# Attention features, then hash-routed experts on one core: each expert's weights loaded one place earlier, and turned outputs joined and scattered three steps later

## The chip, the cores and the metric

The kernel runs on one core of a Trainium2 chip. The metric is the device time of one execution in microseconds (us), as the median of several runs. The engines are named as in the profile: PE (TensorE matmuls), PEld (its weight loads), DVE (VectorE), ACT (ScalarE), POOL (GpSimd) and SP (SyncE, which here only issues DMAs).

## The reference

Two blocks follow each other. The first is attention without a softmax, over 4 batches, 4 heads, 1088 positions and head size 32, all in float32:

```python
def phi(x):
    a = np.einsum('rd,bhsd->bhsr', S1, x)          # r = 8
    b = np.einsum('rd,bhsd->bhsr', S2, x)
    return np.einsum('bhsi,bhsj->bhsij', a, b).reshape(*x.shape[:-1], r * r)
q_p, k_p = phi(q), phi(k)
kv = np.einsum('bhsf,bhsd->bhfd', k_p, v)
z = np.sum(k_p, axis=2)
num = np.einsum('bhsf,bhfd->bhsd', q_p, kv)
den = np.einsum('bhsf,bhf->bhs', q_p, z)[..., None] + 1e-06
x = (num / den).transpose(0, 2, 1, 3).reshape(B * S, H * D)   # 4352 rows of 128
```

The second sends each of the 4352 rows to one of 8 experts by its token id, and runs the expert's two layers (w1 is 128 x 1024, w2 is 1024 x 128):

```python
expert_idx = token_ids * np.int64(2654435761) % np.int64(8)
for e in range(8):
    mask = expert_idx == e
    h = np.maximum(x[mask] @ w1[e], 0.0)
    out[mask] = h @ w2[e]
```

## The kernel before

**Attention.** A loop goes over the four batches `b`. PE turns q and k, multiplies them by S1 and S2, turns the features, and forms kv and the numerators; DVE forms the features (L532), ACT evicts, POOL copies v into place (`values`, L552) and divides (`x_main`, L623; `x_tail`, L629). SP loads q, k and v (`load_main`, L122) and stores the rows of x to a DRAM tensor `x_rows` (`x_rows`, L634; `x_tail_rows`, L638). While `b` is 0 and 1, the routing is computed: `order` (L366) holds the experts by rank, `get` and `put` the rows to gather and to scatter.

**Experts.** The rows of an expert are cut into an early group of 256 (rows of the first two batches) and a late group of 320 or fewer, so there are 16 groups; `by_turn` is the order in which they are worked: 0, 1, 2, 3, 4, 8, 5, 9, 6, 10, 7, 11 to 15. A group takes eight steps `c`, one for each 128 columns of the hidden layer. In a step PE does layer 1 of this group (`layer1`, L918, into one of four PSUM banks), ACT or DVE evicts it with the relu (L648, L650, every other step), and PE does layer 2 of the group ahead (`layer2`, L926). So the step of a group is fixed by PE while the banks come free in time.

**Rows in and out.** `fetch_tile` gathers 128 rows by an indirect DMA from POOL (L642); its index is copied by DVE just ahead (`paced`, L709), which sets when the gather may go. The first tiles are turned on PE (`bring`, L720; `bring_tile`, L726). From the fourth group on, DVE splits the rows into 16-bit halves (`turn_in`, L734), a DMA transpose from SP turns them (L735), and DVE joins them (`join_in`, L740). Outputs go the other way: at the end of a group ACT copies the two halves (`out_columns`, L966), SP issues two DMA transposes one group later (`turn_out`, L979), DVE joins them (`join_out`, L987), and POOL scatters 128 rows at a time by an indirect DMA (`scatter_next`, L929).

**Weights.** `load_expert(r, layers, ahead)` reads the expert of rank r into a register of SP (L135) and loads whole layers (512 KB each, L143 and L147); `ahead` is a small write to the tile, on ACT or DVE, that the load has to wait for, so that it goes no earlier than that engine reaches that point. `load_half` loads half a layer (256 KB) behind a memset of DVE (L155, L159).

**Order.** Every engine works through one queue, in the order in which the program text issues its instructions (a manual schedule). In the expert part the table `beside` gives what is issued next to PE's steps: `at(g, c, f)` puts f behind step c of the group in turn g. For the step of the joins:

```python
for g in range(2, G - 1):
    at(g, 1, turn_out, by_turn[g - 2])
    c = FC if g < E else 5
    for i, f in enumerate((join_out, scatter_next, scatter_next, scatter_next)):
        at(g + (c + i) // FC, (c + i) % FC, f)
```

FC and E are both 8: for g below 8, join_out stands at step 0 of the next group, and the scatters at its steps 1 to 3.

Of the kernel before, what the change touches and what calls it, by code (L numbers as in the profile page):

```python
# [30 lines left out]
def kernel(  # L31
# [17 lines left out]
    E, _, F = moe_w1.shape  # L49
# [10 lines left out]
    FC = F // P  # L60
# [53 lines left out]
    def load_main(src, b, tag, ahead=None):  # L114
        t = load.tile([P, H, T, D], F32, tag=tag, name=f"{tag}{b}")
        if ahead:
            ahead(t[:, 0, 0, 0:1])
        rows = src[b, :, 0:SM, :].rearrange("h (p t) d -> p h t d", t=T)
        parts = {(0, "k"): H, (0, "q"): H, (0, "v"): H // 2}.get((b, tag), 1)
        for i in range(parts):  # L120
            hs = slice(i * H // parts, (i + 1) * H // parts)
            nc.sync.dma_start(t[:, hs], rows[:, hs])  # L122
        return t
# [8 lines left out]
    def load_expert(r, layers=(1, 2), ahead=None, eng=nc.sync, eng_type=ENG.SP):  # L132

        if r not in at_rank:
            _, es = nc.values_load_multi_w_load_instructions(  # L135
                order[0:1, r:r + 1], engines=(eng_type,), min_val=0, max_val=E - 1,
                skip_runtime_bounds_check_because="a count of the experts ahead of one of them is below their number")
            at_rank[r] = es[0]
        e = at_rank[r]
        if 1 in layers:  # L140
            if ahead:
                ahead(w1[:, r, 0:1])
            eng.dma_start(w1[:, r], moe_w1[bass.ds(e, 1)].rearrange("o p f -> p (o f)"))  # L143
        if 2 in layers:
            if ahead and 1 not in layers:
                ahead(w2[:, r, 0, 0:1])
            eng.dma_start(w2[:, r], moe_w2[bass.ds(e, 1)].rearrange("o (c p) d -> p (o c) d", p=P))  # L147
# [195 lines left out]
    def route_bases(cnt):  # L343

        less = const.tile([P, E], F32, name="less")
        nc.vector.scalar_tensor_tensor(less[:], took[:], is_late[:], cnt[:, 0], op0=OP.mult, op1=OP.add)
        base = const.tile([P, E], F32, name="base")
        nc.vector.scalar_tensor_tensor(base[:], place[:], float(1 << RB), less[:], op0=OP.mult, op1=OP.add)
        nc.vector.tensor_tensor(seq[:], seq[:], base[:].unsqueeze(2).to_broadcast([P, E, C]), op=OP.add)
# [66 lines left out]
    def hot(dst, numbers, values):  # L416

        _, n, w = dst.shape
        nc.vector.tensor_tensor(dst.rearrange("p c (n x) -> p c n x", x=2),
                                numbers.rearrange("p (n x) -> p n x", x=2).unsqueeze(1).to_broadcast([P, n, w // 2, 2]),  # L420
                                values.unsqueeze(2).to_broadcast([P, n, w // 2, 2]), op=OP.is_equal)

    def route_rows(part):
        c = slice(part * C // 2, (part + 1) * C // 2)
        hot(row1[:, c], number[:], st[:, 1, c])
# [57 lines left out]
    def turned_all(src, which):  # L483
        sT, half = turned(src, which)
        for g in range(GQ):
            nc.scalar.copy(sT[:, g], half(g)[:])
        return sT
# [93 lines left out]
    def q_turned(f, engs):  # L581

        fT = work.tile([P, T, H // 2, P], F32, tag="fT", name="fT", bufs=1)
        for i, eng in enumerate(engs):
            copy_of(eng)(fT[:, 2 * i:2 * i + 2], f_turned(f, i)[:])
        return fT
# [80 lines left out]
    turn_of = {g: i for i, g in enumerate(by_turn)}  # L667
# [80 lines left out]
    A, V = nc.scalar, nc.vector  # L748
# [50 lines left out]
    for b in range(B - 1):  # L799
        last = b == B - 2  # L800
        if b > 1:
            kT = turned_all(k_t[b + 1], "kT")
        if b == 1:
            q_t.append(load_main(q, 3, "q", A.memzero))
        if last:
            qT = turned_all(q_t[b + 1], "qT")
        fT = q_turned(f, (A, A, A, A) if b > 0 else EVICT)
        if b == 0:
            route_bases(cnt)
            digits = route_ranks()  # L810
            tail_ps = bank([P, 2, TT, P], "tail_ps")
            tail_turned(k_tail, tail_ps, 0)
            tail_turned(q_tail, tail_ps, 1)
            tailT = work.tile([P, 2, TT, P], F32, tag="tailT", name="tailT", bufs=1)
            nc.scalar.copy(tailT[:], tail_ps[:])
            qT = turned_all(q_t[1], "qT")
            for u, va_tail in enumerate(va_tails):
                rows = tail_rows(u * TT)
                nc.gpsimd.tensor_copy(va_tail[rows, :, :, 0:D], v_tail[rows])
            tail_features(tail_products(tailT))  # L820
            route_parts(digits)
            route_order_end()
        elif not last:
            qT = turned_all(q_t[b + 1], "qT")
        if b == 1:
            v_t.append(load_main(v, 2, "v", A.memzero))
            route_in_tile()
        if last:
            idx = route_list()
            route_end(idx)  # L830
        if b > 0:
            kv = kv_products(b, kp, range(T + 1))
            m = kv_diagonal(b, kv)
        if b == 1:
            route_tiles_p()
        if last:
            load_expert(0, (1,), A.memzero)
        abq, aq, f = ab_bank(), first_of_ab(), feature_tile("f")
        s_products(abq, qT, range(GQ))
        first_copied(aq, abq, range(GQ))  # L840
        abk, ak, kp = ab_bank(), first_of_ab(), feature_tile("kp")
        s_products(abk, kT, range(GQ))
        first_copied(ak, abk, range(GQ))
        if b == 0:
            q_t.append(load_main(q, 2, "q", A.memzero))
            kT, half = turned(k_t[2], "kT")
            nc.scalar.copy(kT[:, 0], half(0)[:])
            kv_products(0, None, range(T, T + 1), kv)
            m = kv_diagonal(0, kv)
            tail_f_turned()  # L850
            nc.scalar.copy(kT[:, 1], half(1)[:])
        values(b + 1)
        if b == 1:
            v_t.append(load_main(v, 3, "v", A.memzero))
            route_rows(0)
            route_tiles()
            route_rows(1)
            denominators(0)
            x_main_all(0)
            for g in range(GQ):  # L860
                x_rows(0, g)
            x_tail_rows(0)
        features(f, aq, abq, range(GQ))
        if b == 0:
            route_slots()
        x_products(b, fT, m)
        x_tail_products(b, m)
        if b == 0:
            k_t.append(load_main(k, 3, "k", A.memzero))
        if last:  # L870
            load_expert(0, (2,), A.memzero)
        if b == 0:
            features(kp, ak, abk, range(GQ))
        elif last:
            features(kp, ak, abk, range(GQ))
            denominators(b)
        else:
            denominators(b)
            features(kp, ak, abk, range(GQ))
        if 0 < b and not last:  # L880
            x_main_all(b)
        if b == 1:
            for g in range(GQ):
                x_rows(1, g)
            x_tail_rows(1)
        if last:
            for j in range(tiles_of(0)[1]):
                fetch_tile(0, j, True)

    e = B - 1  # L890
    fT = q_turned(f, EVICT)
    load_expert(1, (1,), A.memzero)
    for j in range(2):
        fetch_tile(1, j)
    kv = kv_products(e, kp, range(T // 2))
# [141 lines left out]
    def at(g, c, f, *a):  # L1037
        beside.setdefault((g, c), []).append(lambda: f(*a))
# [12 lines left out]
    for j in range(tiles_of(1)[1]):  # L1051
        at(0, 5 + j, bring_tile, 1, j)
    at(1, 5, bring, 2)
    for r in range(2, E):
        for x in range(2):
            at(turn_of[r] - 1, 3 * x, load_half, r, 2, x)
            if r > 2:
                at(turn_of[r] - 2, 4 + 3 * x, load_half, r, 1, x)


    ahead = [(k, j) for k in by_turn[4:11] for j in range(tiles_of(k)[1])]
# [3 lines left out]
    assert not ahead  # L1065

    gate = nc.vector.memset
    at(0, 1, load_expert, 1, (2,), lambda x: gate(x, 0.0))
    at(0, 5, load_expert, 2, (1,), lambda x: gate(x, 0.0))
    for i in range(GQ):  # L1070
        at(0, 5 + i, x_main, e, i, nc.gpsimd)
        at(1, 1 + i, x_rows, e, i)
# [7 lines left out]
        at(i - 1, 4, join_in, by_turn[i])  # L1080
    for g in range(2, G - 1):
        at(g, 1, turn_out, by_turn[g - 2])
        c = FC if g < E else 5
        for i, f in enumerate((join_out, scatter_next, scatter_next, scatter_next)):
            at(g + (c + i) // FC, (c + i) % FC, f)
        if g == G - 4:

            at(g, 7, nc.gpsimd.drain)
        if g == G - 3:
            at(g + 1, 0, nc.gpsimd.drain)  # L1090
# [17 lines left out]
    g, lo = G - 1, size_of(G - 1) - P  # L1108
# [40 lines left out]
    with tc.If(turns > 0):  # L1149
        with tc.For_i(0, turns):  # L1150
# [19 lines left out]
            at = moe.tile([P, C], F32, tag="at", name="at", bufs=1)  # L1170
# [70 lines left out]
```

## Time and profile before

| | us |
|---|---|
| median of 3 runs | 178.63 (178.38, 178.63, 179.55) |
| profiled execution, its own time | 180.15 |
| its span | 178.1 |
| PE busy | 170.3 |
| PEld busy | 143.0 |
| DVE busy | 96.2 |
| POOL busy | 93.0 |
| ACT busy | 67.9 |
| DMA, mean | 145 GB/s over the span |

The span goes from the first to the last instruction of the profiled execution; what lies around it belongs to the start and end of the program. Busy times are shares of different stages: attention takes the first 52 us, the expert groups the rest. A row of a timeline gives the start, the duration, the engine, the line, the operation with its output and input, a count, and in brackets the idle time of the engine ahead of it and what ended it. A row of waits gives who waited for whom, the sum in us, how often, and the longest. In a row of windows the numbers are the length, then busy time and count of PE, PEld, DVE, ACT and POOL, the granted PE clock, the DMA share and GB/s.

### The profile page before, as it was taken

To read this page: it belongs to the slowest core of one execution; us is meant where nothing else is said; L and a number is where in the kernel's file an instruction comes from. 1 tells how busy PE (TensorE), PEld (TensorE's weight loads), DVE (VectorE), ACT (ScalarE), POOL (GpSimd) and SP (SyncE) were. 2 spreads that over 40 slices of the span, in tenths; PEclk is the share of its full clock that TensorE was granted. 3 is DMA by queue.
4 is the path that set the end of the run, shared out by engine and by line. 5 is a ranking of instruction groups with operands and counts; after the bars stand their busy time and mean duration, and the time that the engine had idled before them with its cause. 6 is when DMAs were issued, how large, how long until landed. Compare 5 with 4: busy or idle time off the path is not lost. (4 is left out here: it accounts for less than half of the span.)

```text
span 178.1 us, 4354 instructions
## 1 busy us (share of the span) xinstructions
PE 170.3 (96%) x1571; PEld 143.0 (80%) x1571; DVE 96.2 (54%) x311; ACT 67.9 (38%) x183; POOL 93.0 (52%) x134
## 2 busy tenths in 40 slices
PE   7899999999999999699999999999999999999990
PEld 3689999999888888588777778788888777778990
DVE  3688998997944423364444343633457562442330
ACT  3548686846453232132341323133141332321330
POOL 7314342775258465077776612775655760406752
PEclk9999999999999999999999999999999999999997
DMA  4897249554668679894992683386342522210111
GB/s 141 239 279 219 86 137 309 157 196 156 196 233 235 223 183 199 165 289 102 230 170 74 184 173 74 103 216 140 79 96 52 117 65 54 54 37 29 43 36 32
DMA packets 39398, 25.83 MB, mean 145 GB/s; under 512 B 20980, under 2 KB 35573, under 8 KB 39376
## 3 DMA queue, kind: packets, MB, share of 16 engines
q1 hardware_dynamic: 36960, 20.98, 47.5%
q0 software_dynamic: 2240, 4.53, 8.9%
q8 instruction: 13, 0.21, 0.5%
q10 hardware_dynamic: 176, 0.04, 0.1%
q14 instruction: 9, 0.07, 0.1%
HBM read 17.41 MB, written 4.52 MB: 123 GB/s over the span
## 5 line engine op out<-in xcount | busy, mean ns | idle before, releaser
L926 PE MATMUL op<-hT,w 128*128 128x256 f32 (+8 forms) x256 | 76.3, 389 | 0.0
L650 DVE TENSOR_SCALAR hT<-hp 128x256 f32<-128x256 f32 (+9 forms) x68 | 29.1, 428 | 56.2 <-PE hp L918 53.4
L926 PEld LDWEIGHTS op<-hT,w 128*128 128x128 f32 x256 | 47.5, 190 | 10.5
L648 ACT ACTIVATE hT<-hp 128x256 f32<-128x256 f32 (+9 forms) x68 | 26.6, 391 | 64.4 <-PE hp L918 62.7
L929 POOL DMA_INDIRECT out_dram<-os,put x35 | 35.3, 1008 | 28.0 <-DVE os L987 11.4
L642 POOL DMA_INDIRECT xg<-x_rows,idx x33 | 34.0, 1031 | 28.7 <-DVE idx L709 19.0
L918 PE MATMUL hp<-xT_late,w 128*128 128x320 f32 (+8 forms) x144 | 41.7, 385 | 0.0
L918 PE MATMUL hp<-xT,w 128*128 128x256 f32 x128 | 37.7, 382 | 1.6 <-DVE idx L709 1.6
L918 PEld LDWEIGHTS hp<-xT,w 128*128 128x128 f32 x128 | 23.8, 190 | 7.5 <-DVE idx L709 2.0
L918 PEld LDWEIGHTS hp<-xT_late,w 128*128 128x128 f32 x144 | 25.3, 190 | 4.7
L532 DVE TENSOR_TENSOR f<-first_of_ab,ab_ps 128x1024 f32<-128x1024 f32 x8 | 9.3, 1205 | 1.8 <-ACT first_of_ab L525 1.8
L987 DVE COPY os<-turned 128x256 uint16<-128x256 uint16 (+1 forms) x26 | 7.4, 329 | 5.3 <-DMA turned<-half 5.3
L532 DVE TENSOR_TENSOR kp<-first_of_ab,ab_ps 128x1024 f32<-128x1024 f32 x8 | 9.3, 1209 | 0.9 <-ACT first_of_ab L525 0.9
L561 PE MATMUL kv<-va,kp 128*64 128x33 f32 x256 | 8.5, 224 | 0.1
L561 PEld LDWEIGHTS kv<-va,kp 128*64 128x64 f32 x256 | 7.9, 138 | 0.8 <-issue 0.4
L734 DVE COPY xh<-xg 128x256 uint16<-128x256 uint16 (+1 forms) x26 | 7.1, 316 | 2.2 <-DMA xg<-x_rows,idx 2.2
L597 PE MATMUL x_ps<-m,fT 128*64 128x66 f32 x256 | 8.3, 222 | 0.0
L597 PEld LDWEIGHTS x_ps<-m,fT 128*64 128x64 f32 x256 | 7.8, 137 | 0.5 <-issue 0.5
L966 ACT COPY half<-op 128x256 uint16<-128x256 uint16 x16 | 5.2, 375 | 7.5 <-PE op L926 7.5
L578 PE MATMUL fT_ps<-ident,f 128*128 128x128 f32 x64 | 7.9, 275 | 0.0
L552 POOL COPY va<-v 128x1024 f32<-128x1024 f32 (+1 forms) x4 | 3.7, 934 | 7.9 <-DMA v<-in_v_dram 4.1
L578 PEld LDWEIGHTS fT_ps<-ident,f 128*128 128x128 f32 x64 | 7.0, 140 | 0.3
(199 smaller groups left out, 166.3 us busy)
## 6 DMA issues: line engine op xcount, KB each, us to landing
w<-in_moe_w_dram SPq DMA_DIRECT2D x22, 256.0 KB, 4.5
w<-in_moe_w_dram SPq DMA_DIRECT2D x5, 512.0 KB, 5.4
x_rows<-xs SPq DMA_DIRECT2D x8, 256.0 KB, 3.1
k<-in_k_dram SPq DMA_DIRECT2D x3, 512.0 KB, 5.8
q<-in_q_dram SPq DMA_DIRECT2D x3, 512.0 KB, 4.9
v<-in_v_dram SPq DMA_DIRECT2D x3, 512.0 KB
out_dram<-os,put POOLq DMA_INDIRECT x35, 2.6
xg<-x_rows,idx POOLq DMA_INDIRECT x33, 3.5
```

The costliest lines, as they stand in the source:

```text
L532: nc.vector.tensor_tensor(dst[:].rearrange("p t h i j -> p (t h) i j")[:, r], a[:, r].unsqueeze(3).to_broadcast(shape), rows_of_ab(ab)[:, ...
L561: nc.tensor.matmul(kv[h * R * R:(h + 1) * R * R, pr], f[:, 2 * pr + h].rearrange("p i j -> p (i j)"), v_[:, 2 * pr + h], start=(t == 0 and ...
L578: nc.tensor.transpose(p[:, t, pr], f[:, 2 * i + t, 2 * pr:2 * pr + 2].rearrange("p h i j -> p (h i j)"), ident[:])
L597: nc.tensor.matmul(p[r, t, 2 * pr:2 * pr + 2].rearrange("p h d -> p (h d)"), fT[:, lo + t, pr, r], m[:, pr].rearrange("p h d -> p (h d)"), ...
L642: nc.gpsimd.indirect_dma_start(out=dst, out_offset=None, in_=x_dram[0:rows], in_offset=bass.IndirectOffsetOnAxis(ap=idx, axis=0), bounds_c ...
L648: nc.scalar.activation(dst, src, AF.Relu if relu else AF.Copy)
L650: return nc.vector.tensor_scalar(dst, src, 0.0, None, op0=OP.max).ins
L734: nc.vector.tensor_copy(xh[:, x * w:(x + 1) * w], _half(xg3[k][:].rearrange("p a b -> p (a b)")[:, 0:w], x))
L918: nc.tensor.matmul(hp[:, 0:hi - lo], w1[:, g % E, c * P:(c + 1) * P], x_columns(first_of(g) + lo, first_of(g) + hi), start=True, stop=True)
L926: nc.tensor.matmul(ops[g][:, 0:hi - lo], w2[:, g % E, c], hTs[g][:, c, lo:hi], start=(c == 0), stop=(c == FC - 1))
L929: st_ = nc.gpsimd.indirect_dma_start(out=out[:], out_offset=bass.IndirectOffsetOnAxis(ap=idx, axis=0), in_=src, in_offset=None, bounds_che ...
L987: nc.vector.tensor_copy(_half(os[:].rearrange("p a b -> p (a b)"), x)[:, 0:n * DM], tts[x][:, 0:n].rearrange("p a b -> p (a b)"))
```

## The change

The loads of the first experts' layers each take the place in the order where the layer ahead of them was loaded. The first layer of rank 0 has a new place, behind the load of the fourth v, without a gate. Rank 2 is now loaded in two whole layers, and halves begin with rank 3, whose first layer takes steps 0 and 3 of turn 1. Joins and scatters of the outputs with g below 8 go from steps 0 to 3 to steps 3 to 6 of the next group.

```diff
         if last:
-            load_expert(0, (1,), A.memzero)
+            load_expert(0, (2,), A.memzero)
...
         if b == 1:
             v_t.append(load_main(v, 3, "v", A.memzero))
+            load_expert(0, (1,))
             route_rows(0)
...
         if last:
-            load_expert(0, (2,), A.memzero)
+            load_expert(1, (1,), A.memzero)
...
     fT = q_turned(f, EVICT)
-    load_expert(1, (1,), A.memzero)
+    load_expert(1, (2,), A.memzero)
...
-    for r in range(2, E):
+    for r in range(3, E):
         for x in range(2):
             at(turn_of[r] - 1, 3 * x, load_half, r, 2, x)
-            if r > 2:
-                at(turn_of[r] - 2, 4 + 3 * x, load_half, r, 1, x)
+            at(turn_of[r] - 2, (4 if r > 3 else 0) + 3 * x, load_half, r, 1, x)
...
-    at(0, 1, load_expert, 1, (2,), lambda x: gate(x, 0.0))
-    at(0, 5, load_expert, 2, (1,), lambda x: gate(x, 0.0))
+    at(0, 1, load_expert, 2, (1,), lambda x: gate(x, 0.0))
+    at(0, 5, load_expert, 2, (2,), lambda x: gate(x, 0.0))
...
-        c = FC if g < E else 5
+        c = FC + 3 if g < E else 5
```

## The prediction

> **What bounds the kernel now.** I read four views in this order: busy times, waits of TensorE, timelines of the engines around the one long wait, and the DMA row there.
>
> ```profile
> PE 170.3 (96%) x1571; PEld 143.0 (80%) x1571; DVE 96.2 (54%) x311; ACT 67.9 (38%) x183; POOL 93.0 (52%) x134
> ```
> ```profile
> PE hp L918 <- DVE idx L709: 1.6, 1, 1.6
> PE idle L225 <- POOL warm L180: 1.0, 1, 1.0
> PE ab_ps L510 <- ACT qT L756: 0.2, 1, 0.2
> ```
>
> TensorE (PE) is busy in 170.3 of 178.1 us, and its list of waits has three entries, 2.8 us together. In the expert part its matmuls stand at an even step (0.43 us for one of 128x256), so busy is real there. The last matmul begins at 173.3; the 4.5 us behind it are the last copy, the last scatters and their landing. So only one thing can be won inside the program: the 1.6 us wait of L918. The waits view blames an index copy (L709), which takes 0.1 us; the true holder stands two lines ahead of it in VectorE's (DVE's) timeline:
>
> ```profile
> 73.86 0.31 DVE L987 COPY os<-turned 128x256 uint16<-128x256 uint16 x1 [4.67 <-DMA turned<-half]
> 74.34 0.31 DVE L987 COPY os<-turned 128x256 uint16<-128x256 uint16 x1 [0.17 <-DMA turned<-half]
> 74.55 0.42 DVE L650 TENSOR_SCALAR hT<-hp 128x256 f32<-128x256 f32 x1
> ```
> ```profile
> 72.86 0.59 PE L926 MATMUL op<-hT,w 128*128 128x256 f32 x2
> 75.02 0.70 PE L918 MATMUL hp<-xT,w 128*128 128x256 f32 x2 [1.56 <-DVE idx L709]
> ```
> ```profile
> 66.33 2.46 SPq L979 DMA_TRANSPOSE turned<-half  x2
> ```
>
> The first join_out stands at the start of group 3, in VectorE's in-order queue. From 69.2 it waits 4.67 us for the first turned output; behind it are the evictions (L650) that give PSUM banks back. PE lives on its four banks until 73.46, then stands 1.56 us. VectorE could be held for 73.46 - 69.2 = 4.3 us before it cost anything.
>
> Why was that transpose late? It was issued at 66.33 and its reader went on at 73.86, while the queue list gives 2.8 us from issue to landing as the median of these transposes. The DMA view for 70 to 74 us (40 slices of 0.1 us) shows the reason:
>
> ```profile
> DMA  3243949994999199099000000000000006999299
> GB/s 110 82 67 59 243 85 248 205 405 26 70 169 120 41 31 187 0 20 5 0 0 0 0 0 5 5 10 10 10 10 10 10 10 200 292 302 225 26 276 348
> ```
>
> From 72.0 to 73.3 hardly a packet starts although SyncE (SP) has transposes and weights outstanding. All queues stand. I see this once; it is not a load that the order of the code forces.
>
> **How the profiled run stands to the median.** Its own time is 180.15, its span 178.1, so 2.05 us lie around the span. The runs shown have 178.38, 178.63 and 179.55. The profiled one is 1.52 us above the median, and the gap is 1.56 us: the likeliest reading is that the median run has next to no gap, that the 179.55 run has most of it, and that a standstill comes in some executions only. The reading against it: a profiled execution may be longer for its own reasons, and then the median has the gap too. This choice is the largest one in the forecast.
>
> **The change part by part.**
>
> *Join and scatter three steps later.* In groups 3 to 8, L987 and the scatters (L929) go from steps 0 to 3 to steps 3 to 6. In group 3, step 3's L918 is at 71.56; after its eviction, two index copies and the turn_in copies (L734, 0.6 us) the join stands at about 73.1, not 69.2: 3.9 us later. Same instructions, same 0.31 us each; nothing added. Even if the turned output still came at 73.86, VectorE would be held 0.8 us plus 0.5 us for the second half, against 4.3 us that the banks cover: the PE gap goes, -1.56 us. What is late next: join_in of group 4 (L740, now behind the join) must be done before group 4 begins, at 68.97 + 6.9 = 75.9. In the profiled run its transpose was issued at 69.53 and the copies ran at 76.01, but behind the held VectorE; the transpose's median landing (3.4 us) gives 72.9, and with the standstill I estimate 75, so 0 to 0.4 us come back in such a run. On POOL, the gathers that stood behind the held index copies (5.5 us idle until 75.30) issue ahead of the scatters, so its run of back-to-back issues, 1.3 us each until 99.8, gets shorter. Scatters go 2.6 us later. Group 3 has four gathers and two scatters, 7.8 us of POOL in 6.9, so 0.9 us runs over; from group 4 on there are four or five issues, at most 6.5 us, in groups of 6.9 to 7.8, so they fit. The last groups (step 5) are untouched, so the tail does not move by itself.
>
> *Weights one place earlier.* 8.4 MB before and after; whole loads go from 5 to 6, halves from 22 to 20: one SP issue (0.38 us) and two memsets (0.06 us) fewer, both off PE's path. No weight is waited for now (no L918 or L926 wait on w), so arriving earlier is worth nothing directly. Indirectly: the half of expert 3's first layer at 65.24 and its register load leave the place ahead of the first turn_out. By the issue times (0.4 + 0.3 for the load and its gate, 0.5 for the register load, the rest waiting) L979 moves from 66.33 to about 64.8, and 256 KB less are ahead of it. That is a second cover of 1.5 us for the same wait; it cannot be won twice.
>
> *The first load behind the fourth v.* SP issues that v at 31.6 and then stands until 34.34 for POOL's xs. The new register load (0.27 to 0.80 us in the trace; order has been there since 21.4) and one issue (0.34) fit in: 0 us. On the queue, 512 KB now come ahead of x_rows(0) and x_rows(1), whose landing releases the first gather:
>
> ```profile
> 35.00:40.00 5.00, 5.00 (x128) 4.79 (x128) 4.86 (x11) 2.55 (x7) 4.01 (x6) 1.00 0.55 203
> ```
> ```profile
> 41.91 1.29 POOL L642 DMA_INDIRECT xg<-x_rows,get  x1 [1.86 <-DMA x_rows<-xs_tail]
> 43.50 1.00 POOL L642 DMA_INDIRECT xg<-x_rows,get  x1 [0.30 <-issue]
> ```
> ```profile
> 46.81 0.44 PE L720 MATMUL xp<-ident,xg 128*128 128x128 f32 x2
> ```
>
> These 5 us moved 203 GB/s at a DMA share of 0.55 (second number from the end). Adding 512 KB needs 308 GB/s, and the page's row has 309 in its best slice of 4.45 us. So 0 us if the queue takes it. If 203 GB/s were its limit, the 512 KB would take 2.6 us more; the second gather lands near 43.5 + 2.5 = 46.0 and PE needs it at 46.81, so 0.8 us are free and PE would stand 1.8 us. A gain is excluded, PE doesn't wait here. Value 0.1 us (the share is far from 1, and x_rows(1) is issued only at 37.7, when most has drained); ends 0 and +1.8. After that the second layer of expert 0, as large, stands where the first did (40.76), and so on: 0.
>
> *Sum* on the profiled execution: -1.56 + 0.1 + 0 to 0.4 gives about 178.8 of 180.15. On the median, where by my reading the gap is mostly absent, the change removes what lifts some runs above the fastest (178.38): **178.2**, with the few tenths it takes from the spread.
>
> **A rule against the change.** The Trainium skill, Advanced Engine Details and Errata, section X-Bar Transpose (TRN2), has transposes as fast as ordinary DMAs, 350 to 400 GB/s. By it the pair of 64 KB transposes needs an estimated 0.4 us of transfer, the output is there by about 70, VectorE is held 1 us of the 4.3 that are covered, and a later join gains 0. The row says 73.86 and a gain of 1.56. I take the row for the profiled run, but the rule describes the run without a standstill, which I hold for the typical one.
>
> **Rivals.**
> 1. The gap is in the typical run as well. For it: all of it is written out in program order, late transposes recur (L987 waits three times, 5.3 us), and a profile may cost its own 1.5 us. Against it: 1.52 against 1.56. Then 178.63 - 1.56 = 177.1, or down to 176.4 if the shorter POOL backlog and earlier transposes also remove later waits.
> 2. Slower: the early 512 KB delay x_rows, hence the gather, and PE waits at bring(0) (L720 at 46.81). It decides from 0.8 us of delay on. At 203 GB/s: 178.4 + 1.8 = 180.2; if the second layer's 512 KB then also stand in the gather's way, 1 us more, 181. For it: nothing there has more than 0.8 us of slack. Against it: the free DMA share of 0.45.
> 3. It doesn't do what it says: the standstill catches join_in of group 4 or a gather, and PE stands elsewhere. 178.6. For it: 75 against 75.9 is tight.
>
> **How the numbers follow.** Forecast 0.42 (177.8 to 178.8), rival 1 0.33, rival 2 0.15, rival 3 0.10. A measurement here tells about 1% from no change, 1.8 us. Faster by over 1% (below 176.8): two thirds of rival 1 at its lower end and a little of the forecast, 0.25. Slower by over 1% (above 180.4): most of rival 2, its upper part and mishaps on the same path, 0.12. The rest, 0.63, within. The range goes from rival 1's lower end, 176.3, to the entry of rival 2's upper part, 180.3.
>
> **What would show it.** Right: no wait of PE on L918 near 73, L987 of the first output at about 73 and its wait under 1 us, L979 first at about 64.8, the first load of w at about 33, the gather still near 42 and L720 near 46.8 without idle. Wrong: an idle entry ahead of L720 (rival 2); a new PE wait at the start of group 4 (rival 3); unprofiled runs that all fall by 1.5 us (rival 1), which would mean that the gap was in every run and my reading of the 1.52 us was a coincidence.

## The result and the profile after

The change takes 179.47 us (median of 20 runs, 178.67 to 182.72), the kernel before, run beside it, 179.18 (20 runs, 178.38 to 180.43). The ratio is **1.001, interval 0.9989 to 1.003**: no difference. In this ratio and in those below, the few longest runs of a kernel are left out (of the change the four from 181.38 us on). The profiled execution of the change has 179.0 us as its own time and a span of 177.2, against 180.15 and 178.1 before.

The first row of the page after, with the busy time of each engine, and then the list of PE's waits (who waited for whom, sum in us, times, longest):

```profile
PE 170.0 (96%) x1571; PEld 142.9 (81%) x1571; DVE 95.8 (54%) x309; ACT 67.7 (38%) x183; POOL 93.4 (53%) x134
```
```profile
PE idle L225 <- POOL warm L180: 1.0, 1, 1.0
PE s_ps L284 <- DVE s_rep L275: 0.4, 1, 0.4
PE xp L726 <- DMA xg<-x_rows,idx: 0.3, 1, 0.3
PE ab_ps L510 <- ACT qT L756: 0.2, 1, 0.2
```

The 1.6 us that L918 waited for L709 are gone from the list. A new entry stands there: `bring_tile` (L726), which turns the first rows of expert 1, waits 0.3 us for a gather. (The 0.4 us of L284 lie at the start of the program.) Behind line 855 the numbers of the changed kernel are one higher, up to the last groups: L919 is the old L918, L980 the old L979, L988 the old L987. DVE's timeline shows the first join, where the kernel before was held 4.67 us:

```profile
73.07 0.15 DVE L709 COPY idx<-get 128x1 int32<-128x1 int32 x1
73.90 0.52 DVE L988 COPY os<-turned 128x256 uint16<-128x256 uint16 x2
74.32 0.14 DVE L709 COPY idx<-get 128x1 int32<-128x1 int32 x1
```

There is no bracket behind L988: no wait is laid to it. It stands 4 us later in the order, behind the index copies, and its outputs are there. The standstill of the DMA queues is not gone. The DMA view of the change for 68 to 74 us, 40 slices of 0.15 us:

```profile
DMA  0066212599999999990001005995965977999899
GB/s 20 1 164 191 82 34 68 160 283 335 345 335 400 295 227 106 147 41 2 7 9 27 0 3 70 143 243 166 298 96 150 219 218 218 410 437 396 328 369 437
```

From 70.7 to 71.6 hardly a byte moves, as before from 72.0 to 73.3. PE waits for nothing there now. The loss is 20 us earlier. PE's timeline of the kernel before, then of the change, where expert 1's tiles are turned between the matmuls of layer 1:

```profile
51.79 1.99 PE L918 MATMUL hp<-xT,w 128*128 128x256 f32 x8
53.62 0.27 PE L726 MATMUL xp<-ident,xg 128*128 128x128 f32 x1
...
54.27 1.26 PE L918 MATMUL hp<-xT,w 128*128 128x256 f32 x4
```
```profile
51.63 1.99 PE L919 MATMUL hp<-xT,w 128*128 128x256 f32 x8
53.92 0.33 PE L726 MATMUL xp<-ident,xg 128*128 128x128 f32 x1 [0.29 <-DMA xg<-x_rows,idx]
...
54.79 1.26 PE L919 MATMUL hp<-xT,w 128*128 128x256 f32 x4
```

From the eight matmuls to the four behind both turns it is 54.27 - 51.79 = 2.48 us before and 54.79 - 51.63 = 3.16 after: 0.68 us lost, though the list of waits shows only 0.3 of them. The last group of matmuls (L1137), of the kernel before, then of the change:

```profile
171.64 1.95 PE L1137 MATMUL op_rows<-w,hT 128*128 128x128 f32 x16
```
```profile
170.33 1.95 PE L1137 MATMUL op_rows<-w,hT 128*128 128x128 f32 x16
```

From the first L726 to this row there are 118.02 us before and 116.41 in the change. With the joins alone (e1 and e8, below) there are 116.19 in both profiles. So in these profiles the late joins take 1.83 us off this stretch, a little more than the one wait in the list; the weights cost 0.22 of it and another 0.45 ahead of L726 (53.92 - 46.66 against 53.62 - 46.81). The change was 0.15 ahead at L720, and 1.83 - 0.22 - 0.45 + 0.15 = 1.31 us remain between these two executions. The medians show none of it.

### The profile page after: what moved, and what is told of

It is laid out like the page before. It is cut to its first block, busy times and chain, and to the rows that moved or that the text cites. A ratio compares the mean times of both kernels' runs of the same rounds, so it can differ in the third digit from the quotient of the medians.

```text
span 177.2 us, 4349 instructions
## 1 busy us (share of the span) xinstructions
PE 170.0 (96%) x1571; PEld 142.9 (81%) x1571; DVE 95.8 (54%) x309; ACT 67.7 (38%) x183; POOL 93.4 (53%) x134
## 5 line engine op out<-in xcount | busy, mean ns | idle before, releaser
L642 POOL DMA_INDIRECT xg<-x_rows,idx x33 | 34.5, 1047 | 21.3 <-DVE idx L709 12.1
L919 PE MATMUL hp<-xT_late,w 128*128 128x320 f32 (+8 forms) x144 | 41.7, 385 | 0.0
L919 PE MATMUL hp<-xT,w 128*128 128x256 f32 x128 | 37.7, 381 | 0.0
L919 PEld LDWEIGHTS hp<-xT_late,w 128*128 128x128 f32 x144 | 25.3, 190 | 4.7
L919 PEld LDWEIGHTS hp<-xT,w 128*128 128x128 f32 x128 | 23.9, 191 | 5.5 <-ACT hT L648 0.4
L561 PE MATMUL kv<-va,kp 128*64 128x33 f32 x256 | 8.4, 224 | 0.1
L561 PEld LDWEIGHTS kv<-va,kp 128*64 128x64 f32 x256 | 7.9, 138 | 0.8 <-issue 0.4
L597 PE MATMUL x_ps<-m,fT 128*64 128x66 f32 x256 | 8.3, 222 | 0.0
L597 PEld LDWEIGHTS x_ps<-m,fT 128*64 128x64 f32 x256 | 7.8, 137 | 0.5 <-issue 0.5
L988 DVE COPY os<-turned 128x256 uint16<-128x256 uint16 (+1 forms) x26 | 7.3, 324 | 1.6 <-DMA xg<-x_rows,idx 1.0
L734 DVE COPY xh<-xg 128x256 uint16<-128x256 uint16 (+1 forms) x26 | 7.0, 313 | 1.2 <-DMA xg<-x_rows,idx 1.0
```

The source lines that it names most:

```text
L561: nc.tensor.matmul(kv[h * R * R:(h + 1) * R * R, pr], f[:, 2 * pr + h].rearrange("p i j -> p (i j)"), v_[:, 2 * pr + h], start=(t == 0 and ...
L597: nc.tensor.matmul(p[r, t, 2 * pr:2 * pr + 2].rearrange("p h d -> p (h d)"), fT[:, lo + t, pr, r], m[:, pr].rearrange("p h d -> p (h d)"), ...
L642: nc.gpsimd.indirect_dma_start(out=dst, out_offset=None, in_=x_dram[0:rows], in_offset=bass.IndirectOffsetOnAxis(ap=idx, axis=0), bounds_c ...
L734: nc.vector.tensor_copy(xh[:, x * w:(x + 1) * w], _half(xg3[k][:].rearrange("p a b -> p (a b)")[:, 0:w], x))
L919: nc.tensor.matmul(hp[:, 0:hi - lo], w1[:, g % E, c * P:(c + 1) * P], x_columns(first_of(g) + lo, first_of(g) + hi), start=True, stop=True)
L988: nc.vector.tensor_copy(_half(os[:].rearrange("p a b -> p (a b)"), x)[:, 0:n * DM], tts[x][:, 0:n].rearrange("p a b -> p (a b)"))
```

## The experiments

Kernels that are compared ran on one chip, one after the other, with the kernel before among them; there are five such groups. In the first two the kernel before took 179 to 180 us, in the three later ones 190 to 192, and every kernel took longer there. One chip is in both conditions (179.42, and later 190.31). So numbers are compared within a group, and ratios are to the kernel before in the same group.

### First condition: the parts alone

**The joins alone**, twice (e1, e8): in the kernel before

```diff
-        c = FC if g < E else 5
+        c = FC + 3 if g < E else 5
```

> Only the joins and scatters three steps later; weights as before. Theory 'two parts cancel': the late turned output no longer holds VectorE, so the profile has no wait of PE on L918 near 73 and no wait ahead of the expert 1 tiles (L726), and the runs lose the part that lifts them above the fastest: median near 178.6, ratio 0.995 to 0.998. Rival 'cover was enough': the gap near 73 was in few executions, so the median stays at that of before, ratio 0.999 to 1.001. Rival 'joins cost': scatters bunched behind the gathers hold POOL and the ratio is over 1.002.

> Joins and scatters alone once more, for a narrower interval. If the joins remove the lift: 0.995 to 0.999 again, no PE wait in the expert groups. If the first result was chance: 0.999 to 1.002.

Measured: 178.75 against 179.42 (ratio 0.998, interval 0.994 to 1.0019), and on another chip 178.9 against 179.91 (0.9953, 0.9914 to 0.9992). Both profiles have no wait of PE left but the one at the start and one of 0.2 us; this is the whole list of the second:

```profile
PE idle L225 <- POOL warm L180: 1.0, 1, 1.0
PE ab_ps L510 <- ACT qT L756: 0.2, 1, 0.2
```

In the profiles the joins do what the prediction said. In the time they show 0.2 and 0.5%; the first interval holds 1, the second ends just below it. The fastest runs differ less than the medians: 178.22 against 178.29 in the first group, 178.18 against 178.51 in the second. A gap of 1.6 us has no room in those runs of the kernel before, so it is not in every execution.

**The weights alone** (e2): the change with the joins put back.

```diff
-        c = FC + 3 if g < E else 5
+        c = FC if g < E else 5
```

> Only the weights one place earlier; joins as before. 'Two parts cancel': the early load costs 0.3 to 0.7 us where the gathers of expert 1 are waited for (PE L726 near 54, waiting for xg), and the join near 69 to 74 still holds VectorE up to 4 us but its transposes are issued near 65, so PE waits at most 0.5 us there: ratio 1.002 to 1.005. 'Cover was enough': the L726 wait of 0.3 us was one execution's: ratio 0.999 to 1.001, and this profile shows no L726 wait.

Measured: 179.88 (178.65 to 182.77), ratio 1.0024 (0.9988 to 1.006), in the group of e1. In its profile PE has no gap near 73 us, with the joins at their old place: the turned outputs are issued at 64.72 in place of 66.33, and that alone covers the wait in this execution, the fastest of the twelve. DVE's first join there, with no wait:

```profile
69.42 0.31 DVE L988 COPY os<-turned 128x256 uint16<-128x256 uint16 x1
```

The waits at L726 (0.3 to 0.7 us) and near 73 us (up to 0.5) that I had expected are not there either. Yet the median is not lower than before: what the earlier issue wins in this execution does not show in the time, so I looked for a loss.

**Where: expert 1's loads?** e3 is the change with the second layer of rank 1 and all later loads at their old places, so that nothing is loaded beside expert 1's gathers; e4 is the change with a first layer (large packets) in the place behind `q_turned`.

```diff
 # e3
     fT = q_turned(f, EVICT)
-    load_expert(1, (2,), A.memzero)
...
-    at(0, 1, load_expert, 2, (1,), lambda x: gate(x, 0.0))
-    at(0, 5, load_expert, 2, (2,), lambda x: gate(x, 0.0))
+    at(0, 1, load_expert, 1, (2,), lambda x: gate(x, 0.0))
+    at(0, 5, load_expert, 2, (1,), lambda x: gate(x, 0.0))
 # e4
-    load_expert(1, (2,), A.memzero)
+    load_expert(2, (1,), A.memzero)
...
-    at(0, 1, load_expert, 2, (1,), lambda x: gate(x, 0.0))
+    at(0, 1, load_expert, 1, (2,), lambda x: gate(x, 0.0))
```

> The change, but nothing is loaded between expert 1's first layer and the third batch's rows: expert 1's second layer and all later loads stand where they stood before. 'Two parts cancel', by amount of traffic: 512 KB fewer lie beside the gathers of expert 1, PE waits 0.0 us at L726 and the tile matmuls follow the eight L918 ones within 1.9 us: ratio 0.995 to 0.998, the best of these four. If the wait at L726 came by chance: same as the other runs within 0.1%.

> The change, but in the place ahead of the third batch's rows stands the first layer of rank 2 (packets of 4 KB) instead of the second layer of rank 1 (packets of 512 B), which goes to turn 0 step 1. Same bytes in each place. If the gathers of expert 1 are late because of the small packets, L726 waits 0.0 us and the ratio is as in the run with the hole (0.995 to 0.998); if because of the bytes, L726 waits 0.3 us as in the change and the ratio is 1.000 to 1.003.

Measured: 179.56 (ratio 1.0029, 0.9994 to 1.0065) and 179.99 (1.0022, 0.9978 to 1.0066). Neither helped; I had expected e3 to be the best of the four of this group. Neither profile has a wait at L726. Neither has e2, e5 or e7, which load the same in that place as the change, so the wait at L726 is seen once. The profiled execution of e3, the longest of its 13 runs with 185.48 us, has a wait one stage ahead of where I looked: at the first gathers, which `bring` of expert 0 (L720) turns.

```profile
49.20 0.33 PE L720 MATMUL xp<-ident,xg 128*128 128x128 f32 x1
50.92 0.33 PE L720 MATMUL xp<-ident,xg 128*128 128x128 f32 x1 [1.39 <-DMA xg<-x_rows,get]
51.18 1.92 PE L561 MATMUL kv<-va,kp 128*64 128x33 f32 x32
```

The wait is 1.39 us, but what follows costs more. Windows of the same run (length, busy time and count of PE, PEld, DVE, ACT and POOL, then the granted PE clock, the DMA share and GB/s):

```profile
45.00:50.00 5.00, 4.53 (x91) 4.06 (x87) 4.96 (x8) 2.93 (x7) 2.20 (x2) 1.00 0.70 205
50.00:55.00 5.00, 4.08 (x45) 3.53 (x45) 1.80 (x7) 1.04 (x4) 3.03 (x4) 0.61 0.48 155
55.00:60.00 5.00, 5.00 (x75) 4.37 (x74) 0.94 (x4) 2.13 (x6) 0.39 (x1) 0.70 0.07 16
```

The granted clock falls from 1.00 to 0.61 and 0.70 behind the wait: the 32 matmuls of L561 take 1.92 us in place of 1.13. From the first L720 to the first L726 this run takes 60.70 - 49.20 = 11.50 us, the kernel before 6.81: 4.7 us are lost there, 1.39 of them the wait and at most (0.39 + 0.30) x 5 = 3.5 the clock. In the profile of e4 the same line waits 0.50 us.

Not all of the 185.48 us comes from there. At the first L561 this run is already 1.7 us behind the kernel before (12.60 against 10.90), and e4 1.6 (12.48): in both, the first 32 matmuls of L510 take 1.98 us in place of 1.16. No load has been moved so early in the program, so this is not the work of the edits. Two of the ten profiles of this condition begin so, and such starts alone could move the median of twelve runs.

**Where: the first load.** e5 moves it behind the third v, e7 behind the stores of x_rows of batch 1, both in the change; e6 moves only the first load in the kernel before and leaves its old place empty.

```diff
 # e5 (+ behind the third v) and e7 (+ behind the stores of batch 1)
-            load_expert(0, (1,))
 # e6, in the kernel before
-        if last:
-            load_expert(0, (1,), A.memzero)
...
             v_t.append(load_main(v, 3, "v", A.memzero))
+            load_expert(0, (1,))
```

> The change, with the first layer of rank 0 loaded behind the third v (issued near 28) instead of the fourth, so that it moves ahead of the fourth v, where the DMA queue is nearly empty near 31 to 33, and not between the fourth v and the stores of x. Theory 'early load delays the stores of x': from the issue of the last x_rows tail to the first gather 2.7 to 3.0 us as before (3.7 to 4.9 in the change), no wait of PE at L720, ratio 0.995 to 0.999 as for joins alone. Rival 'all later loads do it': gather as late as in the change only if the other moves cause it; ratio 1.001 to 1.004.

> The kernel before, with one move: the first layer of rank 0 behind the fourth v, its old place left empty. 'Early load delays the stores of x': 3.7 to 4.9 us from the last x_rows tail to the first gather, PE waits 0 to 1.4 us at L720 in some executions, ratio 1.002 to 1.005. Rival 'all later loads do it': 2.7 to 3.0 us and a ratio of 0.999 to 1.001.

> The change, with the first layer of rank 0 behind the stores of the second batch's x (issued near 39.5), so that it is early but behind x_rows in the queue; the second layer follows near 41. 'Early load delays the stores of x': 2.7 to 3.0 us from tail to gather, but 1 MB then lies beside the first gathers; L720 waits at most 0.3 us, ratio 0.997 to 1.001. Rival 'amount of traffic beside the gathers': L720 waits 0.5 us or more, ratio 1.002 or more.

Measured: 179.54 (0.9981, 0.9943 to 1.0018), 179.71 (0.9993, 0.9965 to 1.002) and 179.85 (0.9988, 0.9948 to 1.0029), all in the group in which the joins alone (e8) had 178.9. All three wait at L720. The row of each timeline, e5, e6, e7:

```profile
47.77 0.51 PE L720 MATMUL xp<-ident,xg 128*128 128x128 f32 x2 [0.35 <-DMA xg<-x_rows,get]
```
```profile
47.56 0.33 PE L720 MATMUL xp<-ident,xg 128*128 128x128 f32 x1 [0.58 <-DMA xg<-x_rows,get]
```
```profile
48.06 0.33 PE L720 MATMUL xp<-ident,xg 128*128 128x128 f32 x1 [0.92 <-DMA xg<-x_rows,get]
```

Of what I expected, e5 has the ratio, but not the quick release, and PE waits; e6 has the wait but not the ratio; e7 has the quick release, but three times the wait.

Two terms can be read. One is the release: from the issue of the last store of x_rows (L638) to the first gather (L642) it is 2.75 us in the kernel before, 2.99 and 2.84 with the joins alone, but 3.69 in the change, 4.23 in e2, 4.93 in e3, 4.01 in e4, 3.37 in e5 and 3.54 in e6, where 512 KB go ahead of those stores. In e7, where the load goes behind them, it is 3.01. But the stores are issued earlier in most of these (38.28 in the change, 39.16 before), and the first gather of the change starts where it did: 41.97 against 41.91. The other term is the landing. The DMA view gives the first two gathers this median from issue to landing, in the kernel before, the joins alone (e8), the change and e7:

```profile
xg<-x_rows,get POOLq DMA_INDIRECT x2, 2.5
```
```profile
xg<-x_rows,get POOLq DMA_INDIRECT x2, 3.6
```
```profile
xg<-x_rows,get POOLq DMA_INDIRECT x2, 4.4
```
```profile
xg<-x_rows,get POOLq DMA_INDIRECT x2, 4.9
```

It is 3.3 in e2, 3.6 in e3, and 4.2 to 4.8 in e4, e5 and e6. In e7 two loads start beside the gathers, 1 MB, and PE waits 0.92 us, the longest but for e3. Neither term alone puts the waits in order: e2 has a late release and no wait, e7 a quick one and 0.92 us. In e6 nothing large starts beside the gathers until 44.51, and they land late all the same; why stays open. All in all the profiles of this condition have a wait at L720 or L726 in six of seven kernels with the first load moved, and in none of three with it at its old place.

In the time, each kernel's interval meets that of the joins alone. Taken together, the runs of e3 and e4 lie on average 0.77 us above those of e1 (95% interval 0.16 to 1.37), and those of e5 and e7 0.63 above those of e8 (0.05 to 1.20). All four have the late joins, so this is the price of the moved loads; both intervals leave zero out, though not by much.

e6 also bears on a question on which the forecast turned. It has the joins of the kernel before, and its turned outputs are not issued earlier (67.41). The gap is there again, from its list of waits:

```profile
PE hp L917 <- DVE idx L709: 1.0, 1, 1.0
PE xp L720 <- DMA xg<-x_rows,get: 0.6, 1, 0.6
```

### Second condition: the same kernels where all take longer

e9 and e15 have the joins three steps later and the first load behind the third v, its old place empty, so that nothing large starts beside the first gathers; e16 has the first load behind the fourth v instead. e10 has the joins one step later. e11, e13 and e18 are the change, e12 and e14 the joins alone, e17 the kernel before.

```diff
 # e9, e15, in the kernel before, with c = FC + 3
             v_t.append(load_main(v, 2, "v", A.memzero))
+            load_expert(0, (1,))
...
-        if last:
-            load_expert(0, (1,), A.memzero)
 # e16: the same, behind load_main(v, 3, ...)
 # e10, in the kernel before
-        c = FC if g < E else 5
+        c = FC + 1 if g < E else 5
```

> Joins three steps later, the first layer of rank 0 behind the third v (issued near 28 to 29), nothing in its old place near 40.7, all other loads as before: no weights move beside the first two gathers until 44.7. Theory 'weights beside the gathers, not only ahead of the stores, make bring(0) late': no PE wait at L720, ratio 0.994 to 0.998 like joins alone. Theory 'any early load delays the stores of x': gather 3.3 us or more behind the last x_rows tail, L720 waits 0.3 us or more, ratio 0.999 or more.

> The kernel before with the joins one step later instead of three. The hold of VectorE in group 3 begins 0.9 us later than 69.2, against a cover of 4.3 us: a transpose as late as in the profile of before would leave a PE wait on L918 of about 0.7 us, a timely one none. If the gap is what lifts the runs of before, the ratio lies between 1 and that of three steps: 0.996 to 0.999.

> The change itself, beside joins alone on one chip. If the weights give back what the joins win: ratio 0.999 to 1.003, and 0.002 to 0.005 above that of joins alone; the profile may show waits at L720 or L726, 0.3 to 1.4 us. If the weights cost nothing: the same as joins alone within 0.001.

> Joins alone, third time: 0.995 to 0.998 of before and no PE wait in the expert groups, if the first two results hold.

> The change itself, beside the joins alone on one chip. Theory (the two parts cancel): ratio to before 1.000 to 1.003, 0.2 to 0.5% above the joins alone; last tail of x_rows to first gather 3.4 us or more; often a wait of 0.3 to 1 us at L720 or L726. Rival (the joins bring nothing that a typical run shows, and the weights cost nothing): the same ratio as the joins alone, within 0.2%.

> The joins alone (c = FC + 3 in the kernel before). Theory: ratio 0.995 to 0.998; tail to gather 2.7 to 3.0 us; no wait at L720, L726 or at 73 us. Rival: 0.999 to 1.001.

> The joins three steps later and the first load behind the third v, its old place empty: nothing of 512 KB starts beside the first gathers. Theory (the early load delays the release of the gathers, the load beside them delays their landing): release late by about 0.5 us (3.3 to 3.5 us after the tail) but landing quick, so no wait at L720 and a ratio equal to the joins alone within 0.2%. Rival (any early load costs): 0.2 to 0.4% above the joins alone.

> The joins three steps later and the first load behind the fourth v, its old place empty, all other loads as before. Theory (the early load alone makes the release of the gathers late): 3.4 to 3.7 us from tail to gather, a wait of 0 to 0.6 us at L720, ratio 0.1 to 0.3% above the joins alone. Rival (it takes the whole shift of loads): no wait at L720, and the time of the joins alone.

> The kernel before, unchanged, for its profile. Theory (the gap behind the early joins is in the typical execution): a wait of 1.0 to 1.6 us of PE at L918 near 73 to 75 us for DVE idx L709, DVE held over 2 us at L987. Rival (the prediction's own reading: the gap is a rare event, the typical execution has next to none): no PE wait there. If the chip is one on which the kernel before takes some 191 us, the theory expects the same wait and a fall of the granted clock behind it, which makes the difference of 3 to 4 us from the joins alone.

> The change, beside that look at the kernel before. Theory: no wait at 73 to 75 us; ratio 1.000 to 1.003 on a chip where the kernel before takes 178 to 180 us, 0.975 to 0.985 on one where it takes some 191 us. Rival (the change is the same on every chip): 1.000 to 1.003 on either.

| kernel | third group, ratio | fourth group, ratio | fifth group, ratio |
|---|---|---|---|
| kernel before, us | 191.67 | 191.41 | 190.31 |
| the change | 0.9754 (0.9667 to 0.984) | 0.9818 (0.9705 to 0.993) | 0.9767 (0.9698 to 0.9836) |
| joins alone | 0.9769 (0.9711 to 0.9828) | 0.9849 (0.9696 to 1.0002) | |
| joins, first load behind the third v | 0.9796 (0.974 to 0.9851) | 0.9776 (0.9662 to 0.9891) | |
| joins, first load behind the fourth v | | 0.9852 (0.9711 to 0.9994) | |
| joins one step later | 0.988 (0.9793 to 0.9967) | | |

Here the change is about 2% faster than before, and so are the kernels with the joins three steps later (1.5 to 2.5%; two intervals of the fourth group reach 1 or nearly). One step has about half of it, but its interval meets those of three steps. The ratios near 1 that I had expected of e9 to e14 were a miss; that of e18, written after these groups, held (0.975 to 0.985). The medians of the change were 187.88, 186.87 and 184.83 us. Between the kernels with late joins these runs show no difference: the intervals overlap widely, so what I expected of e11 to e16 against each other (0.1 to 0.5%) stays undecided. My expectation of a wait at L720 in the change and e16 was a miss too, as no profile of this condition has one there, and so was that of no PE wait in the expert groups with the joins alone (e12, e14): every profile of this condition has some. Late joins do not even take away every wait for the index copy: L709 is named near 84 to 86 us with 0.48 us in e9, 0.71 in e14 and 1.06 in e16. The release is late in the change here too (4.13, 5.18 and 3.89 us), but PE itself comes later to L720, at 47.21 to 48.78.

e17 is one execution of the kernel before in this condition, of 192.62 us where the group's median is 190.31. It shows what the early joins can cost. DVE and then POOL, from their timelines:

```profile
73.87 0.32 DVE L987 COPY os<-turned 128x256 uint16<-128x256 uint16 x1 [1.62 <-DMA turned<-half]
76.02 0.31 DVE L987 COPY os<-turned 128x256 uint16<-128x256 uint16 x1 [1.83 <-DMA turned<-half]
```
```profile
71.05 0.99 POOL L642 DMA_INDIRECT xg<-x_rows,idx  x1 [0.35 <-issue]
76.98 0.99 POOL L642 DMA_INDIRECT xg<-x_rows,idx  x1 [4.93 <-DVE idx L709]
78.28 1.04 POOL L929 DMA_INDIRECT out_dram<-os,put  x1 [0.30 <-issue]
```

DVE is held twice, the index copy (L709) behind it is late, POOL stands 4.93 us, and from 76.98 on it issues gathers and scatters back to back, 1.3 us each, until 89.9. PE's timeline has the gap at once, and a larger one 15 us later:

```profile
76.70 0.70 PE L918 MATMUL hp<-xT,w 128*128 128x256 f32 x2 [1.01 <-DVE idx L709]
86.30 0.70 PE L918 MATMUL hp<-xT,w 128*128 128x256 f32 x2 [1.56 <-issue]
87.80 0.70 PE L918 MATMUL hp<-xT,w 128*128 128x256 f32 x2 [0.37 <-issue]
92.25 1.44 PE L918 MATMUL hp<-xT_late,w 128*128 128x320 f32 x2 [3.32 <-DMA w<-in_moe_w_dram]
```

The gathered rows of that late group are split (L734) at 87.66, where the kernel before of the first condition has 81.28. The waits view lays the 3.32 us to a weight load; which of the late things ended it is not shown. I had expected the clock to fall behind the gap near 75 us; it stays at 1.00 there and falls behind the second one, in the windows of e17:

```profile
85.00:90.00 5.00, 2.26 (x8) 1.35 (x8) 1.45 (x6) 0.38 (x1) 3.99 (x4) 1.00 0.27 73
90.00:95.00 5.00, 2.75 (x6) 1.98 (x7) 1.20 (x6) 1.64 (x5) 0.00 (x0) 0.60 0.44 135
95.00:100.00 5.00, 5.00 (x17) 3.70 (x16) 1.88 (x9) 0.73 (x2) 2.85 (x3) 0.72 0.34 93
```

e18, the change in the same group, has neither the 1.01 nor the 3.32; its POOL stands 1.90 us at that place. Its first two joins, with no wait:

```profile
75.26 0.50 DVE L988 COPY os<-turned 128x256 uint16<-128x256 uint16 x2
85.66 0.51 DVE L988 COPY os<-turned 128x256 uint16<-128x256 uint16 x2
```

The spans are 190.5 and 182.8, from one execution of each. Of the 7.7 us between them, 1.01 + 3.32 = 4.3 are these two waits, and at most (0.40 + 0.28) x 5 = 3.4 the clock. That both come from the early joins is argued from this one pair. The waits of 1.56 and 0.37, where the profile shows nothing waited for, are not of this kind: e18 has 0.60, 0.33 and 0.34 at L919 from 83.9 on, and the joins alone (e14) 0.9 at L597 near 52, where the first condition has none. Their like stands in every profile of the condition, whatever the kernel; what the condition is stays open.

## Why the prediction was right or wrong

**Right: the mechanism of the joins.** DVE held by L987 lets the banks run out, and joins three steps later end that. L988 came at 73.90 (forecast about 73.1), its wait is gone, L980 was issued at 65.02 (forecast 64.8), and the two covers could not be won twice (e2 and e1 each lose the gap). Late next was join_in of group 4; no profile of the first condition shows PE waiting there, so rival 3 fell.

**The step that failed: the term of the first load, put at 0.1 us.** The sum asked only whether the queue takes 512 KB more ahead of x_rows, and left the gather's landing at the 2.5 us of the kernel before; from these came its 0.8 us of slack at L720. The gather did start near 42 as forecast (41.97), but with the load moved the first two gathers took 4.2 to 4.9 us to land in the change and in e4 to e7, and 3.3 and 3.6 in e2 and e3. PE waits 0.35 to 1.39 us at L720 in five of the seven profiles with the load moved. The change's own profile pays elsewhere, 0.68 us at L726, for gathers issued no later than before (47.82 and 49.38 against 47.98 and 49.54), a place that the sum did not look at. In the time the moved loads take back some 0.6 to 0.8 us, by the averages above; by the ratios 0.3 to 0.5% of 179 us, 0.998 for the joins alone against 1.0029 and 1.0022 for e3 and e4 in one group, 0.9953 against 0.9981 and 0.9988 for e5 and e7 in the other. A mean DMA share of 0.55 over 5 us does not say when one small transfer lands. Rival 2 had the sign, and L720 as the place, where e3 to e7 wait; what it blamed, a late start of the gather, is small in the change's profile. What makes the landing longer is not shown.

**Half wrong: how the profiled run stands to the median.** The step read 180.15 - 178.63 = 1.52 as the gap of 1.56, and concluded that a typical run has next to none. The median of three runs was low: twenty gave 179.18, thirty-five each on two chips 179.42 and 179.91. The joins alone are worth 0.7 to 1.0 us of median (179.42 - 178.75, 179.91 - 178.9; by the ratios 0.4 and 0.8), where the sum gave them "the few tenths it takes from the spread". And the gap came again in every profile that has the old joins without the earlier outputs: 1.56, 0.98 in e6, 1.01 in e17. But all three are executions above their group's median, and the fastest runs of the kernel before have no room for it. So the gap is in some executions, as the step said, but in enough of them to move the median. The standstill of the queues, which it took for a rare event seen once, is none: 17 of the 20 profiles have one between 70 and 79 us (two slices of 0.4 us or more, one behind the other, under 35 GB/s), and the other three (e2, e5, e7) have theirs behind 80. The DMA view of e8, the joins alone, for 68 to 76 us, 40 slices of 0.2 us, where PE waits for nothing:

```profile
DMA  9999993383399993999999990000009949999899
GB/s 286 417 264 177 183 111 105 120 82 54 76 256 304 140 141 110 292 156 248 287 310 229 269 168 10 20 20 22 18 18 345 410 164 348 441 358 328 328 325 340
```

**So the sum was near by luck.** The forecast was -0.4 us on the median shown; measured is +0.3 by the medians and +0.2 by the ratio, within the interval of nothing. Two terms were too small, of opposite sign, and about equal: some -0.4 to -1.0 for the joins, some +0.5 to +0.9 for the loads. In the condition where all kernels take longer, the late joins are worth some 3 to 5 us (1.5 to 2.5% of 190), the second term can't be seen, and the same edit is 2% faster. Why the joins are worth more there is shown by e17 alone.

**The rule against the change.** The rate in X-Bar Transpose (TRN2), on the Trainium skill's page Advanced Engine Details and Errata, would by its estimate have given the joins nothing. Their gain in e8 (0.9953) and in the later groups speaks for the row, 73.86, against that estimate.

**The best version** of those measured in the first condition is the joins alone, in both groups of experiments the lowest median: 178.75 and 178.9. It was not timed beside the change itself in that condition; in the other one the two can't be told apart (0.9769 and 0.9754, 0.9849 and 0.9818).

## What to carry to other kernels

A wait in one profiled run is not shown to be rare, or to be typical, by three unprofiled times: compare the fastest runs as well as the medians of many, and look for the wait in a second profile. When a bulk load is moved earlier, look for the small transfers that PE waits for, and price their landing as well as their start: a mean DMA share has no answer to that. Price a held in-order engine by what queues up behind it on the other engines as well (here the index copies of DVE, and through them 5 us of POOL's gathers); in these runs that part cost time only in e17, where all else was late too.

## What the runs showed of the hardware that I had not expected

- The granted clock can fall behind a short wait: 1.39 us at L720 in e3, then 0.61 and 0.70 for ten us. Behind 3.32 us in e17 it is 0.60 and 0.72. The Trainium skill, TensorE: Matmul & The Clock Gate, section Why this matters for your kernels, advises against idle gaps above some 3 us in mid-kernel; e17 agrees, and e3 fell at less than half of it. The length of the wait alone does not decide: the 1.56 us of the kernel before had no fall (its windows 70 to 75 and 75 to 80 us show 1.00), nor had 1.75 us in e13 (1.00 from 85 to 95 us).
- What lies around the span is not constant: 1.97 to 2.20 us in every run of the kernel before in the first two groups, 1.66 to 1.88 in those of the change and of the joins alone. It is no gain. If the end of the last scatter's issue is taken from the time of the run, 4.87 us remain before (180.15 - 175.28), 5.02 in the change (179.0 - 173.98) and 4.88 with the joins alone (178.36 - 173.48). So spans of different kernels can differ by 0.3 us that the times don't show.
- Whole groups can lie 5 to 12 us higher, for all kernels, and on a chip that was quick some forty minutes before; the granted clock does not tell it (0.995 in e12, of 185.96 us). Only times of one group compare.
